# A tuned gated mix of attention and spectral filter: recalibrated scheduler durations, zero matmuls in TensorE gaps, gate column inside the value projection, 65-row last chunk

## The chip, the cores and the metric

The kernel runs on one core of one Trainium2 chip. Times are device microseconds of a whole execution. Before the change: 541.3 us, the median of three runs (541.14 to 542.06). The profiled span, about 2 us shorter than the time, is that of the traced execution.

Executions of one kernel do not all agree here. Each run comes with a state: "slow" when it is over 1.5% above the fastest run of the same kernel, "fast" otherwise.

## The reference, cut to what matters

```python
x = A_x                                             # 1 x 2048 x 448, bf16
g = sigmoid((x * gate_w).sum(-1, keepdims=True))    # the gate: one number per token
a = attention(x, wqkv, wo)                          # 16 heads of 28
b = irfft2(rfft2(B=x) * (w_r + 1j*w_i))             # over tokens and channels, as matmuls
return g * a + (1 - g) * b
```

The channel dimension of 448 is read by TensorE in four chunks of rows: 128, 128, 128 and 64.

## The kernel before

A scheduler in Python simulates the engines with assumed durations and emits instructions in the order that this simulation gives. The chip then runs each engine's list in order; no time of the simulation is enforced. Attention scores go to two tiles of PSUM of 3 and 2 banks, a bank for the 512 columns of one score matmul (128x1536 and 128x1024 in the profile), and ScalarE takes the exponentials of each (366 large ones). "Background" work (projections, the DFT, and some exponentials as a VectorE polynomial) shares two more banks.

```python
LAT = {"PE": 0.25, "ACT": 0.22, "DVE": 0.12, ...}   # us from an end to the start of a user
SWITCH = 0.17                                       # assumed us between two matmuls of different `mode`
...                                                 # cut
def v_block(self, g, b, due, wop, rel=0.0):         # value projection of 4 x 128 tokens
    for t in range(4):
        for c in range(4):
            n = 128 if c < 3 else 64
            ... mm(bank[:, 112*t:112*t+112], xT[b][0:n, c, 128*t:128*t+128], W[0:n, c, o0:o0+112])
            ops.append(self.pe(112, f, ..., dur=0.065))
...
def gate_item(self, due):                           # 64 matmuls of one column
    for t in range(NT):
        for c in range(4):
            n = 128 if c < 3 else 64
            ... mm(bank[:, t:t+1], xT[t//4][0:n, c, ...], self.wvr[0:n, c, 336:337])
...
e = self.act(0.1 + 512 * len(st) / 1200.0, ...)     # assumed time of one exponential
...
o = self.pe(0, fm, deps, tk + 2.0, mode="col", name="pv", dur=0.27 * len(pair))
```

Three kinds of matmuls alternate, which the code calls modes: scores use 32 rows of the array (`32*128` in the timeline; four heads side by side), the products with V ("PV") 32 columns (`128*32`), and everything else is "full". xT, the transposed input, has a row of ones behind its 448 channels, so its last chunk can be read 65 rows deep; the q and k projections already do that.

The softmax here doesn't subtract the row's maximum and nothing guards it: scores larger than these inputs give would overflow.

## Time and profile before

| | before |
|---|---|
| time, median | 541.3 us |
| profiled span | 537.2 us |
| TensorE busy, ScalarE busy | 89%, 80% |
| mean granted TensorE clock | 0.82 |
| chain of waits | TensorE 44%, VectorE 23%, ScalarE 18% |

These are lines of the profile page of the kernel before: busy time by engine; two rows of the 40 slices of the span (each digit is the busy share, or the granted clock, in tenths); and the chain that ended last.

```profile
PE 475.7 (89%) x3250; PEld 166.4 (31%) x3250; DVE 405.7 (76%) x678; ACT 430.7 (80%) x390; POOL 24.0 (4%) x56
...
ACT  2796777889939978987996987876797788999960
...
PEclk9997555899999968855987575559997996999986
...
PE 44%; DVE 23%; ACT 18%; issue 8%; DMA 4%; SPq 2%; ACTq 0%; DVEq 0%
```

The digits of the clock row fall to 5 in whole groups of slices, and ScalarE's digits are mostly lower there. Next, the windows view of the kernel before (columns: stretch, its length, busy time of each engine with instruction counts, granted clock, DMA share, GB/s):

```profile
40.00:60.00 20.00, 18.78 (x105) 5.15 (x105) 11.38 (x18) 12.98 (x12) 0.25 (x1) 0.68 0.01 2
60.00:80.00 20.00, 20.00 (x100) 5.15 (x100) 8.05 (x14) 14.71 (x13) 0.00 (x0) 0.50 0.06 14
80.00:100.00 20.00, 20.00 (x127) 6.79 (x123) 9.03 (x15) 13.20 (x13) 0.00 (x0) 0.54 0.03 8
140.00:160.00 20.00, 18.51 (x137) 7.49 (x136) 18.91 (x29) 11.89 (x14) 2.04 (x3) 1.00 0.01 4
```

There are two kinds of loss. From 60 to 80 us TensorE is busy for all 20 us at half clock, and ScalarE, which should be the bound, is busy for 14.71. From 140 to 160 us the clock is full, yet ScalarE is busy for 11.89 us only: value and q/k projections hold TensorE.

The timeline of TensorE before (start, duration, engine, line, operation, tiles, shapes, count, and in brackets the idle time before it and what ended it), first around 13 us, then from 37 us on:

```profile
13.02 1.05 PE L465 MATMUL bg<-cst,xtok 128*128 128x128 bf16 x16
...
37.83 1.69 PE L462 MATMUL bg<-wv,xT 128*128 128x112 bf16 x16
...
44.46 0.39 PE L462 MATMUL psA<-q,k 32*128 32x512 bf16 x2 [0.33 <-DMA k<-nrow]
```

Sixteen full-height transposes of 128 columns take 1.05 us; sixteen value matmuls, with fewer columns, take 1.69. The single starts in the trace show where: 49 ns from one 128-row matmul to the next, but about 145 ns into a 64-row one and 152 ns out of it, so some 96 to 103 ns extra each way, called a crossing below. In the same trace the q and k projections, whose last chunk is 65 rows deep, have no such step: at full clock their matmuls of 512 columns start 215 to 227 ns apart, into and out of a 65-row one as between 128-row ones.

### The profile page before, as it was taken

How to read it: one execution, taken by the hardware profiler on the slowest of the kernel's cores; microseconds unless marked ns; L12 is line 12 of the kernel's file. 1: busy time of each engine (PE TensorE's matmuls, PEld its weight loads, DVE VectorE, ACT ScalarE, POOL GpSimd, SP SyncE). 2: the span in 40 equal slices, each digit the busy share in tenths (PEclk: the TensorE clock that was granted, in tenths of full speed). 3: DMA queues.
4: the chain of work that ended last, by engine and by line, in shares of the span. 5: the costliest groups of instructions: out<-in, count | busy, mean ns of one | idle time of the engine just before them, and what ended most of it. 6: DMA issues, size and time to landing. Idle time of an engine off the chain costs nothing.

```text
span 537.2 us, 8484 instructions
## 1 busy us (share of the span) xinstructions
PE 475.7 (89%) x3250; PEld 166.4 (31%) x3250; DVE 405.7 (76%) x678; ACT 430.7 (80%) x390; POOL 24.0 (4%) x56
## 2 busy tenths in 40 slices
PE   7899999999998898799989989997879889888674
PEld 3343223333343322212333332322334333332121
DVE  2534722857989999997998988879896979798422
ACT  2796777889939978987996987876797788999960
POOL 5500000000010000000200000000000000000000
PEclk9997555899999968855987575559997996999986
DMA  8010010021000111111012000000000010010011
GB/s 237 2 55 1 2 23 9 1 56 22 2 4 1 42 42 40 24 34 37 16 23 52 13 1 2 2 10 11 13 13 11 23 29 22 21 36 19 20 35 36
DMA packets 27881, 13.98 MB, mean 26 GB/s; under 512 B 17248, under 2 KB 27456, under 8 KB 27840
## 3 DMA queue, kind: packets, MB, share of 16 engines
q1 hardware_dynamic: 26736, 13.09, 9.4%
q10 hardware_dynamic: 1104, 0.35, 0.3%
q8 instruction: 25, 0.41, 0.3%
q14 instruction: 16, 0.13, 0.1%
HBM read 11.21 MB, written 1.84 MB: 24 GB/s over the span
## 4 chain that ended last, share of the span: by engine, by line
PE 44%; DVE 23%; ACT 18%; issue 8%; DMA 4%; SPq 2%; ACTq 0%; DVEq 0%
PE bg L462 21%; ACT ring L980 18%; PE pvb L462 8%; PE psA L462 7%; PE psB L462 6%; DVE y L916 4%; DVE dW L931 2%; PE bg L465 2%; DVE dW L938 2%; SPq L444 2%; DVE y L942 2%; DVE dF L923 1%; DVE dW L927 1%; DMA k<-nrow 1%; DVE q L755 1%
## 5 line engine op out<-in xcount | busy, mean ns | idle before, releaser
L980 ACT ACTIVATE ring<-psA 128x1536 bf16<-128x1536 f32 (+1 forms) x184 | 274.1, 1490 | 52.3 <-PE psA L462 27.8
L980 ACT ACTIVATE ring<-psB 128x1024 bf16<-128x1024 f32 x183 | 195.3, 1067 | 20.1 <-PE pvb L462 7.1
L462 PE MATMUL psA<-q,k 32*128 32x512 bf16 x550 | 86.9, 451 | 26.0 <-ACT ring L980 23.6
L462 PEld LDWEIGHTS <-k 32*128 32x128 bf16 x1024 | 47.9, 93 | 155.2 <-issue 142.7
L916 DVE TENSOR_SCALAR y<-bg 128x512 uint16<-128x512 f32 x108 | 72.2, 683 | 20.6 <-PE bg L462 17.9
L462 PE MATMUL psB<-q,k 32*128 32x512 bf16 x366 | 84.2, 448 | 3.8 <-ACT ring L980 2.1
L462 PE MATMUL pvb<-ring,vw 128*32 128x512 bf16 x916 | 84.6, 458 | 1.3 <-DVE pvs L1070 0.7
L462 PE MATMUL bg<-q,k 32*128 32x512 bf16 x108 | 46.0, 447 | 3.8 <-DVE y L916 1.7
L462 PEld LDWEIGHTS <-xT 128*128 128x128 bf16 (+1 forms) x384 | 28.0, 101 | 43.4 <-issue 34.7
L938 DVE TENSOR_TENSOR dW<-dW,dF 128x2048 f16<-128x2048 f16 x27 | 32.9, 1217 | 0.2
L931 DVE TENSOR_TENSOR dW<-dF,dW 128x2048 f16<-128x2048 uint16 x27 | 32.8, 1216 | 0.2
L462 PEld LDWEIGHTS <-vw 128*32 128x32 bf16 x1024 | 19.4, 101 | 43.5 <-issue 39.9
L942 DVE TENSOR_TENSOR y<-y,dW 128x2048 uint16<-128x2048 uint16 x27 | 32.7, 1213 | 0.1
L462 PE MATMUL bg<-R,X 128*113 128x256 bf16 x128 | 31.2, 344 | 0.5 <-DVE U L1174 0.2
L462 PE MATMUL bg<-wvr,xT 128*128 128x112 bf16 (+3 forms) x256 | 30.1, 216 | 0.6 <-ACT w L810 0.3
L1174 DVE CAST U<-bg 113x512 bf16<-113x512 f32 x32 | 21.9, 687 | 7.3 <-PE bg L462 6.9
L815 POOL CAST vw<-w 128x16 bf16<-128x16 f32 x16 | 9.8, 628 | 388.4 <-ACT w L810 388.4
L1149 DVE CAST X<-bg 128x450 bf16<-128x450 f32 x16 | 10.0, 626 | 20.7 <-PE bg L462 20.7
L462 PE MATMUL bg<-Bd,xT 128*128 128x450 bf16 x64 | 25.4, 483 | 0.3 <-DVE y L916 0.2
L462 PE MATMUL bg<-xT,wpq 128*128 128x512 bf16 (+1 forms) x60 | 21.4, 447 | 2.2 <-DVE q L755 1.9
L462 PEld LDWEIGHTS <-X 128*113 128x113 bf16 x128 | 16.7, 157 | 19.5 <-issue 19.2
L462 PE MATMUL bg<-xT,wpk 128*128 128x512 bf16 (+1 forms) x60 | 20.6, 435 | 0.7 <-DVE y L916 0.4
(92 smaller groups left out, 458.8 us busy)
## 6 DMA issues: line engine op xcount, KB each, us to landing
RB<-cRB SPq DMA_DIRECT2D x16, 128.0 KB
Wg<-in_B_w_i_dram SPq DMA_DIRECT2D x32, 56.2 KB
xtok<-in_A_x_dram SPq DMA_DIRECT2D x4, 448.0 KB
out_dram<-fin SPq DMA_DIRECT2D x16, 112.0 KB
CS<-cCS SPq DMA_DIRECT2D x16, 96.0 KB
Wg<-in_B_w_r_dram SPq DMA_DIRECT2D x16, 56.2 KB
r<-rhl SPq DMA_DIRECT2D x32, 4.0 KB
U<-in_A_wqkv_dram SPq DMA_DIRECT2D x2, 252.0 KB
```

The source lines that it names most:

```text
L444: self.pin(e.dma_start(out=out() if callable(out) else out, in_=in_() if callable(in_) else in_))
L462: self.pin(self.nc.tensor.matmul(out, lhsT=lhsT, rhs=rhs, start=start, stop=stop, **kw))
L465: self.pin(self.nc.tensor.transpose(out=out, in_=in_, identity=self.c("ident")[0:n, 0:n]))
L755: self.pin(nc.vector.tensor_scalar(out=dst, in0=self.bgi(it), scalar1=self.sv, scalar2=None, op0=ALU.mult))
L815: self.pin(nc.gpsimd.tensor_copy(out=free_dims(self.vw[g][:], [[128, 4], [32, 4]], 4 * b * 128 + DH), in_=self.w[g][:, 4 * b:4 * b + 4, :]))
L916: self.pin(nc.vector.tensor_scalar(out=ys[:, s, :], in0=self.bgi(it), scalar1=127 * UNITS + 1.5, scalar2=0.0, op0=ALU.add, op1=ALU.max))
L931: self.pin(nc.vector.tensor_tensor(out=fl(self.dW), in0=fl(self.dF), in1=fl(self.dW), op=ALU.mult))
L938: self.pin(nc.vector.tensor_tensor(out=fl(self.dW), in0=fl(self.dW), in1=fl(self.dF).bitcast(F16), op=ALU.mult))
L942: self.pin(nc.vector.tensor_tensor(out=fl(ys), in0=fl(ys), in1=fl(self.dW), op=ALU.add))
L980: self.pin(nc.scalar.activation(out=self.ring[:, u0:u0 + len(st), :], in_=slot[:, 0:len(st), :], func=ACT.Exp, scale=LN2 / UNITS))
L1149: self.pin(nc.vector.tensor_copy(out=self.X1[:, t, :], in_=self.bgi(it)[:, 0:F2]))
L1174: self.pin(nc.vector.tensor_copy(out=dst, in_=src))
```

## The change

The intent, as the code shows it: give the simulation durations nearer the chip's; put zero matmuls ("fillers") on TensorE where the simulation finds it idle and its busy share of the last 3.4 us under 0.62; take the gate as a 113th column of one value block; and read the last chunk 65 rows deep, with a zero row in the weights, so that the crossings between 128-row and 64-row matmuls go.

```diff
-LAT = {"PE": 0.25, "ACT": 0.22, "DVE": 0.12, "POOL": 0.15, "SP": 2.1, "AQ": 2.1}
-SWITCH = 0.17
+LAT = {"PE": 0.26, "ACT": 0.22, "DVE": 0.15, "POOL": 0.15, "SP": 2.1, "AQ": 2.1}
+SWITCH = 0.1
+HAMW, HAMF = 3.4, 0.62
@@ the scheduler's loop @@
+        def fill(t):
+            gap = 0.35
+            so = scores.get(nexts)
+            if so is not None and ndep[so] == 0:
+                gap = min(gap, rdy[so] - t)
+            n = min(512, int((gap - SWITCH) * 2400.0) // 32 * 32)
+            if n < 96 or share(t) >= HAMF:
+                return False
+            ...                     # into a free background bank, or added into the open PV sum
                 if best is None:
+                    if e == "PE" and t > 8.0:
+                        f = fill(t)
@@ the filler @@
+        if bank is None:
+            self.mm(self.pv[:, 0:n], self.zero[:, 0:P], self.zero[:, 0:n], False, False)
+        else:
+            self.mm(self.bgt[bank][:, 0:n], self.zero[:, 0:P], self.zero[:, 0:n], True, True)
@@ value block (and the first DFT likewise) @@
-                n = 128 if c < 3 else 64
+                n = 128 if c < 3 else 65
-                ops.append(self.pe(112, f, deps + ops[-1:], due - 1.5, dur=0.065, ...
+                ops.append(self.pe(112, f, deps + ops[-1:], due - 1.5, dur=0.052, ...
+        m = 113 if g == 1 else 112          # the gate column rides in group 1
@@ gate_item: the 64 matmuls are gone, four small copies by VectorE collect the column @@
@@ exponentials, PV products @@
-            e = self.act(0.1 + 512 * len(st) / 1200.0, ...
+            e = self.act(0.052 + 512 * len(st) / 1200.0, ...
-                o = self.pe(0, fm, deps, tk + 2.0, mode="col", name="pv", dur=0.27 * len(pair))
+                o = self.pe(0, fm, deps, tk + 2.0, mode="col", name="pv", dur=0.225 * len(pair))
```

The instruction listing after the change holds 85 fillers with 36,288 columns (15.1 us at the 2.4 columns per ns that the code assumes). The first stands after 224 of the 916 score matmuls; 20 stand behind the last one.

More of the change, by code (lines that the diff above doesn't have):

```diff
@@ L249, in run, with share @@
         dq = list(dunits)
+        pvopen = [False]
+        pebusy = []
+        self.nfill = 0
+        def share(t):
+            a = t - HAMW
+            while pebusy and pebusy[0][1] <= a:
+                pebusy.pop(0)
+            return sum(e - max(s, a) for s, e in pebusy) / HAMW
+        def fill(t):
[6 more added lines that the diff above has]
+                return False
+            bl = [b for b in range(nbg_tiles) if held[b] is None and banks[b] <= t + 1e-9]
+            if bl:
+                target = bl[0]
+                banks[target] = t + SWITCH + n / 2400.0
+            elif pvopen[0]:
+                target = None
+            else:
+                return False
+            o = Op("PE", n / 2400.0, lambda: self.filler(target, n), (), 0.0, 0.0, "full", None, None, None, "fill")
+            o.start = t + (SWITCH if mode not in (None, "full") else 0.0)
+            o.end = o.start + o.dur
+            order.append(o)
+            pebusy.append((o.start, o.end))
+            self.nfill += 1
+            return o.end
         def finish(o, t0, dur):
             nonlocal left
+            if o.eng == "PE":
+                pebusy.append((t0, t0 + dur))
+                if o.name == "pv":
+                    pvopen[0] = not o.n
             o.start, o.end = t0, t0 + dur
@@ L295, in run @@
                 if best is None:
+                    if e == "PE" and t > 8.0:
+                        f = fill(t)
+                        if f:
+                            free[e], mode = f, "full"
+                            progress = True
                     continue
@@ L372, in build @@
         self.background()
+        self.sc.filler = self.filler
         order = self.sc.run(2, self.dunit_ops, 1)
@@ L396, in alloc @@
         self.wvr = T([P, 4, 337], BF16, "wvr")
+        self.WV0 = {1: 0, 2: 113, 3: 225}
         self.wo_pad = [T([P, D], BF16, f"wo{g}") for g in range(4)]
@@ L499, in plan_steps @@
             T.append(t)
-            t += 0.1 + 512 * len(st) / 1200.0
+            t += 0.052 + 512 * len(st) / 1200.0
         self.T, self.Tend = T, t
@@ L646, in weights @@
         K = -4000.0
-        self.wvd = {0: self.wload(self.wv0, 2 * D, 0, 112, K, "SP")}
+        z1 = self.pool(0.05, lambda: self.pin(nc.gpsimd.memset(self.wv0[64:65, 3, :], 0.0)), (), -4600)
+        z2 = self.pool(0.05, lambda: self.pin(nc.gpsimd.memset(self.wvr[64:65, 3, :], 0.0)), (), -4450)
+        self.wvd = {0: self.wload(self.wv0, 2 * D, 0, 112, K, "SP") + [z1]}
         for b in range(1, 4):
@@ L662, in weights @@
             rw[w] = [d1, d2]
-        dv = self.wload(self.wvr, 2 * D, 112, 336, K + 11, "SP", lat=4.0)
-        g1 = self.dma(self.wvr[:, 0:3, 336:337], self.gw[0:384].rearrange("(c p o) -> p c o", p=P, o=1), (), K + 12,
+        dv = (self.wload(self.wvr[:, :, 0:112], 2 * D, 112, 112, K + 11, "SP", lat=4.0)
+              + self.wload(self.wvr[:, :, 113:337], 2 * D, 224, 224, K + 11.5, "SP", lat=4.0))
+        g1 = self.dma(self.wvr[:, 0:3, 112:113], self.gw[0:384].rearrange("(c p o) -> p c o", p=P, o=1), (), K + 12,
                       dur=0.3, lat=8.0)
-        g2 = self.dma(self.wvr[0:64, 3, 336:337], self.gw[384:448].rearrange("(p o) -> p o", o=1), (), K + 12.1,
+        g2 = self.dma(self.wvr[0:64, 3, 112:113], self.gw[384:448].rearrange("(p o) -> p o", o=1), (), K + 12.1,
                       dur=0.2, lat=8.0)
         for g in range(1, 4):
-            self.wvd[g] = dv + [g1, g2]
+            self.wvd[g] = dv + [g1, g2, z2]
         for g in range(1, 4):
@@ L698, in bgi, with filler @@
         return t if dt == F32 else t.bitcast(dt)
+    def filler(self, bank, n):
+        if bank is None:
+            self.mm(self.pv[:, 0:n], self.zero[:, 0:P], self.zero[:, 0:n], False, False)
+        else:
+            self.mm(self.bgt[bank][:, 0:n], self.zero[:, 0:P], self.zero[:, 0:n], True, True)
     def x_block(self, b, due):
@@ L824, in v_block, with fg @@
         W = self.wv0 if g == 0 else self.wvr
-        o0 = 0 if g == 0 else 112 * (g - 1)
+        o0 = 0 if g == 0 else self.WV0[g]
+        m = 113 if g == 1 else 112
         for t in range(4):
             for c in range(4):
-                n = 128 if c < 3 else 64
+                n = 128 if c < 3 else 65
                 def f(t=t, c=c, n=n):
-                    self.mm(self.bgi(it)[:, 112 * t:112 * t + 112], self.xT[b][0:n, c, 128 * t:128 * t + 128],
-                            W[0:n, c, o0:o0 + 112], c == 0, c == 3)
+                    self.mm(self.bgi(it)[:, m * t:m * t + m], self.xT[b][0:n, c, 128 * t:128 * t + 128],
+                            W[0:n, c, o0:o0 + m], c == 0, c == 3)
                 deps = [self.xev[b, cc] for cc in range(4)] + self.wvd[g] + [wop[0]]
-                ops.append(self.pe(112, f, deps + ops[-1:], due - 1.5, dur=0.065, acq=it if not ops else None, rel=rel))
+                ops.append(self.pe(112, f, deps + ops[-1:], due - 1.5, dur=0.052, acq=it if not ops else None, rel=rel))
+        pre = []
+        if g == 1:
+            def fg():
+                self.pin(nc.vector.tensor_copy(out=self.glog[:, 4 * b:4 * b + 4],
+                                               in_=free_dims(self.bgi(it), [[m, 4]], 112)))
+            pre = [self.dve(0.08, fg, ops[-1:], due - 1.5)]
+            self.glops.append(pre[0])
         def fe():
-            src = self.bgi(it)[:, 0:448].rearrange("p (t s d) -> p t s d", t=4, s=4)
+            src = free_dims(self.bgi(it), [[m, 4], [DH, 4], [1, DH]])
             wv = free_dims(self.w[g][:], [[4, 4], [1, 4], [0, DH]], 16 * b)
@@ L840, in fe @@
                                              in0=src, in1=wv, op=ALU.mult))
-        e = self.dve(0.56, fe, [ops[-1], wop[0], self.vms[g], ("vwar", g)], due - 1.5, free=it)
+        e = self.dve(0.54, fe, [ops[-1], wop[0], self.vms[g], ("vwar", g)] + pre, due - 1.5, free=it)
         self.vready[g, b] = [e, wop[1]]
@@ L845, in gate_item @@
         nc = self.nc
-        it = Item()
-        ops = []
-        for t in range(NT):
-            for c in range(4):
-                n = 128 if c < 3 else 64
-                def f(t=t, c=c, n=n):
-                    self.mm(self.bgi(it)[:, t:t + 1], self.xT[t // 4][0:n, c, 128 * (t % 4):128 * (t % 4) + 128],
-                            self.wvr[0:n, c, 336:337], c == 0, c == 3)
-                deps = [self.xev[3, 3]] + self.wvd[1]
-                ops.append(self.pe(64, f, deps + ops[-1:], due, dur=0.06, acq=it if not ops else None, rel=due - 10))
-        e = self.act(0.15, lambda: self.pin(nc.scalar.activation(out=self.ge[:], in_=self.bgi(it)[:, 0:NT],
-                                                                func=ACT.Exp, scale=-1.0)), ops[-1:], -9.0, free=it)
+        e = self.act(0.08, lambda: self.pin(nc.scalar.activation(out=self.ge[:], in_=self.glog[:], func=ACT.Exp,
+                                                                 scale=-1.0)), self.glops, -9.0)
         a = self.dve(0.09, lambda: self.pin(nc.vector.tensor_scalar(out=self.ge[:], in0=self.ge[:], scalar1=1.0,
                                                                     scalar2=None, op0=ALU.add)), (e,), due)
-        b = self.dve(0.12, lambda: self.pin(nc.vector.reciprocal(out=self.gs[:], in_=self.ge[:])), (a,), due)
+        b = self.dve(0.16, lambda: self.pin(nc.vector.reciprocal(out=self.gs[:], in_=self.ge[:])), (a,), due)
         self.gate_op = self.dve(0.09, lambda: self.pin(nc.vector.tensor_scalar(
@@ L869, in attention @@
         self.vready = {}
+        self.glops = []
         rate = (ts[1] - ts[0]) / 16.0
@@ L981, in fe @@
                                               func=ACT.Exp, scale=LN2 / UNITS))
-            e = self.act(0.1 + 512 * len(st) / 1200.0, fe, [m] + exps[-1:], i * .001, name="exp")
+            e = self.act(0.052 + 512 * len(st) / 1200.0, fe, [m] + exps[-1:], i * .001, name="exp")
             e.step = i
@@ L1021, in fm @@
                                     pi == 0 and qi == 0, last and qi == len(pair) - 1, tile_position=(0, 32 * s))
-                o = self.pe(0, fm, deps, tk + 2.0, mode="col", name="pv", dur=0.27 * len(pair))
+                o = self.pe(0, fm, deps, tk + 2.0, mode="col", name="pv", dur=0.225 * len(pair))
+                o.n = pi == len(pairs) - 1
                 prev_pv = o
@@ L1124, in background @@
         dI = self.dma(free_dims(self.Binv[:], [[D, 4], [1, D]]), dr["Binv"].ap(), (), -98, rel=40.0, lat=5.0)
-        self.gate_item(60.0)
+        self.gate_item(ts[4] + 5.0)
         cost = 0.0
@@ L1139, in background @@
             for c in range(4):
-                n = 128 if c < 3 else 64
+                n = 128 if c < 3 else 65
                 def f(c=c, n=n, t=t, it=it):
```

## The prediction

> **What bounds the kernel now.** 541.3 us on one core; the profiled span is 537.2. ScalarE's exponentials are the floor: 366 of them, in a steady full-clock stretch one pair (3+2 banks) per about 2.3 us, so some 415 us plus about 16 us of start and 16 us of tail. They last from 15.5 to 521 us: some 90 us are lost (page: ScalarE 80% busy, TensorE 89%; chain of waits: TensorE 44%, ScalarE 18%). Two causes. (1) The granted clock averages 0.82; the windows view shows only 1.00 and 0.50, some 190 us at half. From 52 to 96 us TensorE is busy without a break at 0.50 and ScalarE only about 70% of the time. A bank of exponentials costs about 0.52 us at full clock, 0.62 at half. (2) Group changes even at full clock: at 152 to 160 us three value projections and the q/k projections hold TensorE for about 8 us while ScalarE waits; smaller holes at 39, 372 and 405 us.
>
> [...]throttled stretches last whole multiples of 3.41 us. Weighing matmul columns by used rows and columns, I estimate that the clock falls after windows under about 0.35 of full-clock capacity, and comes back only after a window over about 0.75 of half-clock capacity: the same work per window.
>
> **What the change does.**
> - 65-row last chunk. Timeline: sixteen 112-column value matmuls take 1.69 us; sixteen 128-row transposes 1.05. Single starts: 49 ns inside 128-row runs, about 145 into and 148 out of a 64-row matmul. With 65 rows I expect the 64-row penalty gone: about 0.19 us for each of 64 value groups and 16 first-DFT tiles, so 15 us of TensorE time; a value block falls to about 0.9 us.
> - Gate column. 64 one-column matmuls go (about 4 us with their switches, in the throttled, TensorE-bound stretch at 60 to 72 us); four small VectorE copies come.
> - Fillers. 85 zero matmuls stand in the new order, 60 in the body (about 10 us at full clock, 2%), 25 around the tail; none before a quarter of the scores, so the throttle of 48 to 98 us has none. Zero data warmed the clock in the prologue. Nothing paces a filler: it runs when reached, so tail fillers run early.
> - New durations reorder work.
>
> **On the critical path.** About half of the 19 us of removed TensorE time (10 us). Throttling at half clock costs about 0.10 us on each of 291 banks, 29 us; I expect half the throttled time to go, 14 us, partly by fillers, partly because the same columns in less time are denser.
>
> **Prediction: 516 us, 8 in 10 between 498 and 533.** Faster by over 2%: 0.83; within 2%: 0.13; slower: 0.04.
>
> **Right if:** value blocks at about 0.9 us; the hole near 152 us about 3 us shorter; mean clock about 0.9; ScalarE's busy share about 84%. **Wrong step shown by:** clock still near 0.82 (fillers misplaced, since the scheduler's full-clock times are not the chip's); TensorE waits in front of fillers; value blocks still 1.7 us.
>
> **What would make it wrong.** Removing slow switches leaves TensorE idler and throttles it more; a new order that is worse in VectorE-bound stretches (160 to 215 us, VectorE 96% busy); or the clock staying full, giving under 500.

The windows of the estimate are stretches of 3.41 us of the trace before. 541 us, less 10 and less 14, is 517, given as 516. What it says of zero data in the prologue, in numbers: in the trace before, ten zero matmuls of 512 columns start from 1.31 us on, 427 ns apart, transposes follow at 5.55 us, and the full clock begins at 6.19 us. In the trace after, eight of the ten and no other matmul had started on TensorE when the full clock began, at 4.62 us; the last two start 217 ns apart.

## The result, and the profile after

483.58 us, median of four runs (482.0 to 486.83), against 541.22 for the kernel before in the same rounds. The ratio is 0.8944, with a 95% interval of 0.8885 to 0.9003. Ratios here are the mean time of one kernel's fast runs over that of the other's of the same rounds, so not quite the ratio of the medians. The change is faster by over 10%, and the time lies below the predicted range of 498 to 533.

| | before | after |
|---|---|---|
| profiled span | 537.2 us | 482.2 us |
| ScalarE busy | 80% | 88% |
| mean granted clock | 0.82 | 0.943 |
| sixteen value matmuls | 1.69 us | 0.98 us |
| end of the last exponential to the end | 16.0 us | 17.4 us |

The same lines of the page after:

```profile
PE 425.6 (88%) x3271; PEld 156.5 (32%) x3271; DVE 401.2 (83%) x682; ACT 423.8 (88%) x390; POOL 22.5 (5%) x58
...
ACT  2679999779999969999999989689999979999950
...
PEclk9989999759999958999999999599999999999998
...
ACT 38%; PE 28%; DVE 15%; issue 13%; DMA 4%; SPq 2%; ACTq 0%; DVEq 0%
```

The chain has turned over: ScalarE 38% and TensorE 28%, where TensorE had 44 and ScalarE 18. The windows view after, at the same times (the value projections of the second group, from 153 us on before, now run from about 123 to 145 us):

```profile
40.00:60.00 20.00, 18.41 (x157) 6.37 (x155) 13.27 (x23) 19.25 (x19) 0.25 (x1) 1.00 0.02 3
60.00:80.00 20.00, 18.81 (x130) 5.89 (x129) 17.46 (x28) 20.00 (x19) 0.00 (x0) 1.00 0.18 44
80.00:100.00 20.00, 18.25 (x110) 4.24 (x107) 13.15 (x24) 17.01 (x15) 0.00 (x0) 0.75 0.02 2
120.00:140.00 20.00, 18.08 (x194) 8.96 (x196) 16.12 (x29) 20.00 (x22) 0.91 (x3) 1.00 0.08 16
140.00:160.00 20.00, 16.75 (x157) 7.16 (x156) 19.97 (x40) 20.00 (x20) 0.80 (x1) 1.00 0.09 20
```

The half-clock stretch of 47 to 98 us (score matmuls 55 to 130) is gone, although no filler stands there; a shorter one comes later in the program, at 90 to 107 us (score matmuls 150 to 175). ScalarE is busy without a break through the group change where it had lost over 7 us. In the value blocks after, the single starts at full clock are 49 ns into a 65-row matmul and 53 ns out of it: the crossings have gone. TensorE's timeline after, a value block, then some fillers:

```profile
239.16 0.98 PE L508 MATMUL bg<-wvr,xT 128*128 128x112 bf16 x16
```

```profile
218.36 0.25 PE L508 MATMUL bg<-zero 128*128 128x192 bf16 x1
218.74 0.39 PE L508 MATMUL psB<-q,k 32*128 32x512 bf16 x2
219.06 0.82 PE L508 MATMUL bg<-zero 128*128 128x512 bf16 x3
220.08 0.39 PE L508 MATMUL psA<-q,k 32*128 32x512 bf16 x3 [0.20 <-ACT ring L1033]
220.41 0.28 PE L508 MATMUL bg<-zero 128*128 128x256 bf16 x1
221.00 0.39 PE L508 MATMUL psB<-q,k 32*128 32x512 bf16 x2 [0.31 <-ACT ring L1033]
221.32 0.98 PE L508 MATMUL bg<-zero 128*128 128x512 bf16 x4
222.34 0.40 PE L508 MATMUL psA<-q,k 32*128 32x512 bf16 x3
```

Here the fillers fall into time in which TensorE would have waited for ScalarE: the scores behind two of the four groups still wait 0.20 and 0.31 us for an exponential, and those behind the other two start within 0.15 us.

### Two readings of the traces that the experiments use

**The clock fell after stretches with few columns.** In the traces before and after, only the clocks 1.00 and 0.50 occur, and every half-clock stretch but the last, which the end cuts off, lasts a whole number of 3.41 us (1 to 15 before, 1 to 5 after), and so does every full-clock one. I cut the traces at that grid and counted, in each window of 3.41 us, the matmul columns, weighed by the share of array rows and columns in use (a measure of mine; some matmul records are missing). Before: of 11 windows after which the clock fell during the exponentials, 10 had at most 0.35 of the full-clock capacity; of 82 at full clock after which it stayed, 3 had. (The traces of a_nofill, a_fill16 and b_dur_65, below, counted in the same way, give 38 falls, all after windows of at most 0.39 and 34 of them of at most about 0.35.) The clock mostly came back after windows of about 0.7 or more of half-clock capacity, which is about the same number of columns, though such a window did not always suffice: a recount of the trace before gives 11 windows after which it came back, 10 of them at 0.69 to 0.97, and 43 after which it did not, 11 of them at 0.69 to 0.75. In the longest half-clock stretch, 51 us from 47 us on, TensorE was busy for all of the 38 us from 60 to 98 us. No long idle gap was needed: the clock fell at 47 us although the longest idle gap of TensorE in the window before was the 0.33 us shown above. In the trace after, about ten windows (9 to 11, by how a matmul across a border is counted) stayed at full clock that would have been under 0.355 without the fillers' columns.

**Two numbers per run.** Each run lists its span and its mean clock, so its time at half clock is 2 x (1 - clock) x span: 193 us in the profile before, 55 after (the half-clock stretches of the two traces add up to 195 and 56). A straight line with one slope for all kernels and one intercept for each fits the 155 runs that list a clock with a spread of 0.7 to 2.7 us per kernel. (One run of the kernel before is left out: its listed clock of 0.677 does not fit its time of 535.9.) The slope is 0.29 us of time per us at half clock. Fast and slow runs of one kernel lie on the same line (they differ by 0.3 us on average), and so do the runs of the kernel before on all four chips (within 1 us). But the slope is not the same for all: the 50 runs of the kernel before alone give 0.24, the kernels built on the changed one 0.34 together, with standard errors of 0.01. The intercept, "time at an equal clock" below, is an estimate worked out from these runs with the common 0.29; it is a way to put a number on what is left when the clock is taken out. Between kernels with about the same half-clock time it hardly depends on the slope; where two differ by 100 us of half-clock time, a slope of 0.24 or 0.34 instead shifts their difference by 5 us either way.

### The profile page after: what moved, and what is told of

The parts are those of the page before. It is cut to its first block, busy times and chain, and to the rows that moved or that the text cites. A ratio compares the mean times of both kernels' runs of the same rounds, so it can differ in the third digit from the quotient of the medians.

```text
span 482.2 us, 8537 instructions
## 1 busy us (share of the span) xinstructions
PE 425.6 (88%) x3271; PEld 156.5 (32%) x3271; DVE 401.2 (83%) x682; ACT 423.8 (88%) x390; POOL 22.5 (5%) x58
## 4 chain that ended last, share of the span: by engine, by line
ACT 38%; PE 28%; DVE 15%; issue 13%; DMA 4%; SPq 2%; ACTq 0%; DVEq 0%
ACT ring L1033 37%; PE bg L508 13%; PE psA L508 5%; PE pvb L508 5%; PE psB L508 4%; DVE y L969 2%; SPq L490 2%; PE bg L511 2%; DVE dW L984 1%; DMA k<-nrow 1%; DMA U<-in_A_wqkv_dram 1%; DVE dF L976 1%; DMA r<-rhl 1%; DMA rs<-pvs 1%; DVE pvs L1124 1%
## 5 line engine op out<-in xcount | busy, mean ns | idle before, releaser
L1033 ACT ACTIVATE ring<-psA 128x1536 bf16<-128x1536 f32 (+1 forms) x184 | 283.8, 1542 | 22.7 <-PE psA L508 16.4
L1033 ACT ACTIVATE ring<-psB 128x1024 bf16<-128x1024 f32 x183 | 205.6, 1124 | 6.9 <-PE pvb L508 4.2
L508 PE MATMUL psA<-q,k 32*128 32x512 bf16 x550 | 76.9, 400 | 25.6 <-ACT ring L1033 22.0
L508 PE MATMUL psB<-q,k 32*128 32x512 bf16 x366 | 75.3, 397 | 6.7 <-ACT ring L1033 5.3
L508 PE MATMUL pvb<-ring,vw 128*32 128x512 bf16 x916 | 73.4, 400 | 0.5 <-DVE pvs L1124 0.5
L508 PEld LDWEIGHTS <-xT 128*128 128x128 bf16 x320 | 18.5, 97 | 16.1 <-issue 14.3
L810 DVE TENSOR_SCALAR k<-bg,cst 128x512 bf16<-128x512 f32 x15 | 11.2, 749 | 13.7 <-PE bg L508 13.7
L1160 DVE SCALAR_TENSOR_TENSOR fin<-bg,gs,xtok 128x448 bf16<-128x448 f32 x16 | 10.9, 680 | 10.9 <-PE bg L508 10.8
L508 PE MATMUL bg<-Bd,xT 128*128 128x450 bf16 x64 | 17.2, 357 | 2.1 <-DVE X L1203 1.0
L976 DVE TENSOR_SCALAR dF<-y 128x2048 uint16<-128x2048 uint16 x27 | 18.5, 686 | 0.3
```

The source lines that it names most:

```text
L508: self.pin(self.nc.tensor.matmul(out, lhsT=lhsT, rhs=rhs, start=start, stop=stop, **kw))
L810: self.pin(nc.vector.tensor_scalar(out=dst, in0=self.bgi(it), scalar1=self.sv, scalar2=None, op0=ALU.mult))
L976: self.pin(nc.vector.tensor_scalar(out=fl(self.dF), in0=fl(ys), scalar1=511, scalar2=None, op0=ALU.bitwise_and))
L1033: self.pin(nc.scalar.activation(out=self.ring[:, u0:u0 + len(st), :], in_=slot[:, 0:len(st), :], func=ACT.Exp, scale=LN2 / UNITS))
L1160: self.pin(nc.vector.scalar_tensor_tensor(out=fin[:], in0=self.bgi(it)[:, 0:D], scalar=self.gs[:, t:t + 1], in1=self.bm[:, t, 0:D], op0=AL ...
```

## The experiments

The scheduler's order is sensitive: a change of 0.002 us in one assumed latency moves 3,000 lines of the order. So, wherever possible, an edit was made at emission only, and the listing was compared to be sure that nothing else moved ("same order"). Theories at the start: "switch" (the 64-row crossings), "clock" (the fillers), "order" (the new durations).

Summary. "Fast ratio" is against the kernel before of the same rounds, given where at least two fast runs exist. Half-clock time and time at an equal clock are means over all runs of the kernel.

| kernel | runs | time, us | fast ratio | half clock, us | at an equal clock, us |
|---|---|---|---|---|---|
| before | 50 | 530 to 551 | | 204 | 480.2 |
| before, 65 rows (b_65) | 4 | 524 to 544 | | 215 | 475.0 |
| before, new durations (b_dur) | 4 | 526 to 548 | 0.978 | 209 | 470.7 |
| before, both (b_dur_65) | 6 | 505 to 524 | 0.947 | 168 | 461.5 |
| after, fillers of 16 columns (a_fill16) | 6 | 501 to 514 | 0.942 | 163 | 461.0 |
| after, no fillers (a_nofill) | 4 | 491 to 512 | | 154 | 459.1 |
| after, no fillers, 64 rows (a_64_nofill) | 6 | 516 to 526 | 0.969 | 178 | 468.2 |
| after, 64 rows (a_64) | 4 | 491 to 512 | 0.915 | 84 | 473.4 |
| after | 4 | 482 to 487 | 0.894 | 63 | 465.6 |

### b_65: the kernel before with 65 rows, same order

```diff
-                n = 128 if c < 3 else 64      # value blocks and first DFT
+                n = 128 if c < 3 else 65      # and row 64 of wv0, wvr set to zero
```

> The kernel before, same order of instructions on TensorE, with the last chunk of the value projection and of the first DFT read 65 rows deep instead of 64 (the extra weight row is zero). Theory 'switch' (the 64-row penalty sat on the chain of waits and is worth about its full TensorE time): 541 falls to 520 to 528, sixteen value matmuls take about 0.9 us instead of 1.69. Theory 'clock' (fillers carry the gain): under 8 us gained here, 533 to 541. Theory 'order' (the new durations carry it): the same, 533 to 541.

Measured: 523.61, 541.61, 542.54 and 543.8 us. The one fast run has a clock of 0.848; the others 0.78 to 0.785. At an equal clock it gains 5 us of the 15 us of crossings, and the half-clock time does not fall. The one fast run lies in the range that "switch" named, but by its clock: at 0.848 the lines of the kernel before (slopes 0.29 and 0.24) give 526 to 529 us. The "switch" theory as stated fails: in the old order most of the freed TensorE time is not kept.

### b_dur: the kernel before with the new durations alone

```diff
-SWITCH = 0.17
+SWITCH = 0.1
-... dur=0.065 (value matmul) ... 0.1 + (exponential) ... dur=0.27 (PV)
+... dur=0.052 (value matmul) ... 0.052 + (exponential) ... dur=0.225 (PV)
```

(LAT and two VectorE durations as in the change.)

> The kernel before with the new durations in the scheduler alone: no filler, 64 rows, gate matmuls kept. Theory 'order': most of the 58 us comes here, 541 falls to 500 to 510. Theory 'switch': little or nothing, since the new durations of a value matmul are true only with 65 rows: 532 to 545. Theory 'clock': 532 to 545, mean clock stays near 0.82.

Measured: 525.93, 526.45, 526.48 (fast) and 547.59 us; fast ratio 0.9779. About 12 us, so neither "nothing" nor "most". The clock is no better (0.814 in the fast runs); at an equal clock it is 9.5 us.

### a_nofill: the changed kernel without fillers, same order

```diff
-            o = Op("PE", n / 2400.0, lambda: self.filler(target, n), ...
+            o = Op("PE", n / 2400.0, lambda: None, ...
```

> The changed kernel with the same order of all other instructions, the 85 fillers left out. Theory 'clock': most of the gain goes, 515 to 540, and the clock falls from 0.94 to about 0.85. Theories 'switch' and 'order': the fillers are worth at most a third, 484 becomes 486 to 503.

Measured: 490.71, 501.53, 511.64 and 511.88 us at clocks of 0.887 to 0.826. The median, 506.58, is 23 us above the changed kernel (the best run, the only fast one by the rule, 7 us), and the executions scatter by 21 us where the changed kernel's scatter by 5. That lies between the two expectations (515 to 540, and at most 503): the fillers carry a large part, not most. The clock is what "clock" expected. With one fast run this is weak by itself; a_fill16 below, with three, settles it.

### a_64: the changed kernel with 64 rows, same order and fillers

> The changed kernel, order and fillers the same, with the last chunk back at 64 rows. Theory 'switch': 484 becomes 500 to 515. Theories 'clock' and 'order': 484 becomes 486 to 495, since TensorE has room at full clock.

Measured: 491.0, 493.95, 493.97 (fast) and 512.23 us. The fast runs are about 10 us above the changed kernel, as "clock" and "order" expected; at an equal clock 7.8. Sixteen value matmuls are back at their old time, in the timeline of this kernel:

```profile
236.93 1.70 PE L508 MATMUL bg<-wvr,xT 128*128 128x112 bf16 x16
```

### b_dur_65: the kernel before with new durations and 65 rows

The same order as b_dur, with the 65-row edit of b_65.

> The kernel before with the new durations and 65 rows, in the same order as the run with the new durations alone; gate matmuls kept, no fillers. At an equal clock I expect 7 to 10 us less than the run with the new durations alone (526): fast runs 510 to 519. If 65 rows were worth their full 15 us and gave clock too: under 508. If the gate column carries much, this stays over 10 us slower at an equal clock than the changed kernel without fillers (489 at 0.887, 500 at 0.848).

Measured: 504.79 to 512.01 (five fast), 524.08 us; fast ratio 0.9465. Against b_dur, in the same order, the 65 rows give 9.2 us at an equal clock and 40 us less at half clock (20 to 25 us less in the changed order, a_64 and a_64_nofill). So the two parts work together. A likely reason, not shown by itself: the new durations say that a value matmul takes 0.052 us; measured, it is 0.061 with 65 rows (0.98 us for sixteen) and 0.106 with 64 (1.69). And this kernel is within about 2 us of the changed kernel without effective fillers (next), which bounds what the gate column and the rest give.

### a_fill16: the same fillers, 16 columns each

```diff
-lambda: self.filler(target, n)
+lambda: self.filler(target, 16)
```

> The changed kernel, same order, every one of the 85 fillers still there but streaming 16 columns instead of 96 to 512: the instructions, their weight loads and their few waits stay, the array activity goes. If fillers work by activity alone (clock theory): like the kernel without fillers, fast runs 490 to 510, clock 0.83 to 0.89. If they work in some other way (as spacers, by the waits they carry): near 484, clock near 0.93.

Measured: 500.97 to 513.55 us, median 509.44; clock 0.827 to 0.86. All 85 instructions, weight loads and waits are there, and the gain is not. It is the columns that count: 163 us at half clock, against 63 with the full columns, all of them zeros, in the same order. The clock rows of the pages: this kernel's (a slow execution at 0.829), and that of b_dur_65 (a fast one, also at 0.829):

```profile
PEclk9999999999995957565755655669999969999887
```

```profile
PEclk9959976999996597978755759896999869697887
```

In the first, the clock holds over the first twelve slices, in which the changed kernel has almost no fillers either, and then breaks down for half the span, where the changed kernel's row above shows nines with a few short falls.

### a_hamf75 and a_hamf90: more fillers

```diff
-HAMW, HAMF = 3.4, 0.62
+HAMW, HAMF = 3.4, 0.75        # 167 fillers;   0.90: 288 fillers
```

> The changed kernel with the filler threshold at 0.75 of the window instead of 0.62: 167 fillers instead of 85, and an order that differs. Theory 'clock' with room left: mean clock 0.95 or above, half-clock time from 55 to about 30 us, time 474 to 482. If fillers cost more TensorE time than they save: 484 to 490 at a higher clock.

> The same with the threshold at 0.90: 288 fillers. If the clock is all that matters: clock 0.97 or above and 468 to 478. If fillers now stand in the way of score matmuls (each up to 0.21 us, no pacing): slower than with 167, 480 to 490, with a high clock.

Measured: 469.0 to 484.16 us (median 474.12, fast ratio 0.8787) and 471.74 to 476.89 us (median 475.07, fast ratio 0.8858). Half-clock time 39 and 17 us, time at an equal clock 463.7 and 469.6 us. Both beat the kernel before and, by their medians, the changed kernel by about 9 us; the interval of a_hamf75's ratio (0.8695 to 0.8879) lies just below the changed kernel's, that of a_hamf90 (0.8787 to 0.8928) overlaps it. Both have another order than the changed kernel, and another order alone moves the median by up to 7 us (a_pert2, below): the fall of the half-clock time, 63 to 39 to 17 us, goes with the fillers, but a gain of 9 us is hardly more than luck of the order. The second expectation of a_hamf90 (slower, by more of them standing in the way) came only in part: at an equal clock it is about 6 us above a_hamf75, in another order, and it gets them back in clock. Its six runs scatter by 5 us, those of a_hamf75 by 15. The clock row of its page (fast, span 475.1):

```profile
PEclk9999999999999999999977987999999999999999
```

### a_64_nofill: no fillers and 64 rows, the changed kernel's order

> The changed kernel, same order, without fillers and with 64 rows: what is left of the change is the order (new durations) and the gate column. Half-clock time 160 to 200 us. If 65 rows are worth the same with and without fillers (7 to 10 us at an equal half-clock time): 512 to 520 at 170 us of half clock, against 507 to 512 without fillers at 65 rows. If the 64-row switches were mostly hidden: under 511.

Measured: 516.27 to 526.4 us, fast ratio 0.9693, 178 us at half clock. Against a_nofill, the 65 rows are worth 9.1 us at an equal clock without fillers, against 7.8 with them (a_64): the expectation of 7 to 10 held.

### b_gate: the kernel before without 48 of the 64 gate matmuls

The gate is wrong on purpose here (and the output was reported wrong); the order of all else is the same.

```diff
-                    self.mm(... self.wvr[0:n, c, 336:337], c == 0, c == 3)
+                    if c == 0:
+                        self.mm(... self.wvr[0:n, c, 336:337], True, True)
```

> The kernel before, same order, with 48 of the 64 gate matmuls left out (the gate is wrong on purpose, from the first 128 of 448 products; all 16 of its 64-row matmuls are among those left out). They stand on TensorE between 56 and 72 us, at half clock, where it is never idle. Theory of the prediction: 3 to 4 us less at an equal half-clock time, 534 to 538. If the removed time is lost again (later in the group or in the clock): 538 to 545, no change.

Measured: 534.54 to 547.2 us, fast ratio 1.0014 (0.9903 to 1.0125). At an equal clock 1.2 us less, which is inside the scatter. The 3 to 4 us are not shown.

### a_pert1 and a_pert2: another order for no reason

```diff
-LAT = {"PE": 0.26, ...       and       "DVE": 0.15
+LAT = {"PE": 0.262, ...      and       "DVE": 0.148
```

> The changed kernel with one assumed latency 0.262 us instead of 0.26: no better information, but another order (3,900 lines of the order listing differ) and 84 fillers. It measures what luck of the order is worth. If the gain is the mechanism's: 478 to 494. If this order was a lucky one: over 500.

> The same with VectorE's assumed latency 0.148 instead of 0.15, 75 fillers. If the gain is the mechanism's: 478 to 494, the clock 0.91 to 0.95. If this order was a lucky one: over 500, the clock below 0.9.

Measured: 473.47 to 490.62 us (median 485.05; one fast run by the rule, since its best run is far ahead) and 483.22 to 499.02 us (median 490.39, fast ratio 0.9066). At an equal clock 465.0 and 461.8, against 465.6; half-clock time 67 and 100 us against 63. So luck of the order is worth up to about 4 us at an equal clock and some 40 us of half clock the other way; between the medians that leaves 7 us. The gain is not luck, but its last 7 us or so may be.

### b_pert1 and b_durx: scatter and parts of the old order

```diff
-LAT = {"PE": 0.25, ...
+LAT = {"PE": 0.252, ...                             # b_pert1
-... 0.1 + (exponential), dur=0.27 (PV)
+... 0.052 + (exponential), dur=0.225 (PV)           # b_durx, nothing else
```

> The kernel before with one assumed latency 0.252 instead of 0.25: another order (3,000 lines of the listing differ) for no reason. If the order's scatter is small: 533 to 547, on the line of the kernel before within 4 us. If the scatter is as large as the 9 us put down to the new durations, that gain is not shown.

> The kernel before with only the durations of exponentials (0.1 to 0.052 us overhead) and of PV products (0.27 to 0.225 us) new. If these carry the order's 9 us: fast runs 524 to 532 at 195 us of half clock. If the latencies, the mode-change time and the value block matter as much: 532 to 540.

Measured: b_pert1 536.07 to 549.99 us, fast ratio 1.0011, 0.7 us under the kernel before at an equal clock. b_durx 536.84 to 556.13 us, fast ratio 1.0066, 4.3 us above it. The exponential and PV durations alone do not give b_dur's 9.5 us, and cost something. Which of the new durations do (latencies, mode-change time, value block, or all together) is open.

### b_fill and b_fill512: unplanned fillers in the old order

```diff
             self.mm(slot[:, e, :], ... scores ...)
+            if i % 2 == 0 and self.pvopen:       # 156 times
+                self.mm(self.pv[:, 0:256], self.zero[:, 0:P], self.zero[:, 0:256], False, False)
```

(512 columns in b_fill512.)

> The kernel before, same order, with 156 zero matmuls of 256 columns (16.6 us at full clock), one after every second group of score matmuls while the PV sum is open: fillers that no scheduler has planned. If the clock itself costs 0.29 us per us at half clock in the old order too: half-clock time falls from 206 to 80 to 150 us and the time from 540 to 515 to 532, on a line about 5 us above the kernel before's (480 + 0.29 x half-clock time). If the price is only 0.15: 535 to 545. If unplanned fillers cost their full time: 545 to 560.

> The same with 512 columns (33 us of TensorE time at full clock). Clock price 0.29: half-clock time under 80 us, time 500 to 522, line some 10 to 15 us above. Clock price 0.15 or full filler cost: 540 to 560.

Measured: b_fill 534.97 to 554.98 us, fast ratio 1.0015. The clock rose (149 us at half, from 204), and the time did not fall: at an equal clock it is 17.7 us above the kernel before, about the full 16.6 us of its filler columns (16.8 at the 216 ns per 512 columns of the trace after). My 5 us were wrong by a factor of three. b_fill512: 523.37 to 548.11 us, fast ratio 0.9789, 110 us at half clock, 24 us above at an equal clock, of 33 us of columns. Within b_fill alone, its seven runs have a slope of 0.29 (0.24 in the kernel before), so time at half clock has a price of that order in the old order as well. The fillers of the changed kernel, placed where the scheduler saw a gap, cost 4.6 us (465.6 against 461.0 of a_fill16) for 15.1 us of columns; with slopes of 0.24 to 0.34 that is nothing to 9 us, so it is below the full price, and not known better.

### a_notail and a_75_notail: no fillers behind the last scores

> The changed kernel, same order, without the 20 fillers after the last score matmul. If they stand in the way: the stretch from the last exponential to the end falls from 17.4 to 15.5 to 16.5 us, the time by about 1 us. If they keep the clock up for the last output matmuls: the stretch grows by 1 us or more. Either way the time is within 2 us of the changed kernel's at an equal half-clock time.

> Threshold 0.75 and no tail fillers. 468 to 477, as the run with threshold 0.75 within 2 us; half-clock time 25 to 65 us as there. Faster than the changed kernel by 6 to 14 us.

TensorE's timeline at the end of the changed kernel shows what was at stake:

```profile
465.14 2.33 PE L508 MATMUL bg<-zero 128*128 128x512 bf16 x10
471.33 0.39 PE L508 MATMUL bg<-r,cst 8*128 8x512 bf16 x1 [3.86 <-DMA r<-rhl]
471.65 1.34 PE L508 MATMUL bg<-zero 128*128 128x512 bf16 x4
472.78 3.10 PE L508 MATMUL bg<-wo,q 128*128 128x448 bf16 x8
```

The ten fillers meant to bridge the wait for the DMA run at once, and TensorE then stands idle for 3.86 us. Measured: a_notail 481.35 to 493.4 us, fast ratio 0.9054; the stretch after the last exponential is 16.9 us instead of 17.4. a_75_notail 471.46 to 490.57 us, fast ratio 0.8992, worse than a_hamf75 by its median (485.98 against 474.12) through more half-clock time (65 against 39 us) at the same 464 us. Leaving the tail fillers out is no gain that these runs show, and a_75_notail missed its expectation. Its order is that of a_hamf75 but for the tail; why its runs have more half-clock time is open (the scatter of executions alone may be it).

## Why the prediction was wrong

The direction, the two causes and most signs were right, and the sum was short by more than half: 25 us predicted, 58 measured. The signs it named came, stronger than named: value blocks at 0.98 us, a clock of 0.926 to 0.943 (0.9 named), ScalarE 88% busy (84% named), and no hole left in ScalarE at the group change. What it listed as the way to be wrong, "the clock staying full, giving under 500", is nearly what happened.

The sum as measured, on the path before, b_dur, b_dur_65, a_fill16, after (means over all runs; the parts are estimates from the fitted lines):

| step | time at an equal clock | half-clock time, times 0.29 |
|---|---|---|
| new durations | -9.5 us | +1.3 us |
| 65 rows | -9.2 us | -11.8 us |
| gate column and the rest | -0.5 us | -1.7 us |
| fillers' columns | +4.6 us | -29.0 us |
| sum | -14.6 us | -41.2 us |

How a step divides between the two columns depends on the slope: with 0.24 the sums are about -22 and -34 us, with 0.34 about -8 and -48. The fast ratios of the same kernels (0.978, 0.947, 0.942, 0.894) need no slope: new durations 12 us, 65 rows 17, gate column and the rest 2, fillers' columns 26, of 541.

- **The step that failed: the price and the amount of throttled time.** The prediction said: "Throttling at half clock costs about 0.10 us on each of 291 banks, 29 us; I expect half the throttled time to go, 14 us". The runs show 0.24 us (the kernel before alone) to 0.29 us (all kernels) for each us at half clock, so some 49 to 59 us for the 204 us of before, and 141 us of it gone, 69%: 34 to 41 us where the prediction had 14. Both factors were too small; the price was 29 us over some 180, or 0.16 per us. The likely error, by the numbers of the traces, was in the baseline. I compared a bank of exponentials at half clock (0.62 us) with the average at full clock in the same trace (0.52), but that average held the group-change holes: at full clock the median time from one exponential to the next is 0.452 us per bank in that very trace. The changed kernel's full-clock stretches run at 0.471 per bank. ScalarE's own floor, which the code's new durations put at 512/1200 + 0.052/2.5 = 0.447 us (an estimate, close to the steady pair of five banks per 2.3 us in the trace before), gives 0.17 us on each of 291 banks: 50 us over 180 us, or 0.28 per us, inside what the runs show.
- **Fillers.** That they count by their columns was right (a_fill16: 163 us at half clock with 16 columns each, 63 with all), and that they would be few and cheap. That half of the throttling would go was an unsupported guess: I had estimated from the trace before that the clock falls under 0.35 of capacity, but did not ask how far below it the windows were. They are just below, most of them 0.26 to 0.35, so by estimate a few hundred columns make up the difference (at 216 ns per 512 columns, 3.41 us hold about 8,090, and 0.05 of that is about 400).
- **65 rows.** The 15 us of crossings and half of them on the path were right: 7.8 to 9.2 us at an equal clock in the changed order. A value block of 0.9 us was nearly right (0.98). Missed: with the new durations it also takes 40 us off the half-clock time (20 to 25 in the changed order); in the old order it does not.
- **Gate column.** Predicted as 4 us of TensorE time of the 19, with half of the 19 on the path. b_gate shows nothing beyond scatter.
- **New durations.** The prediction gave them no number. They are worth 9.5 us at an equal clock, more than three changes of the order for no reason moved it (0.6, 3.8 and 0.7 us), though a part of them alone (b_durx) made it 4.3 us worse.
- **Tail.** The prediction gave it no number; the stretch behind the last exponential grew by 1.4 us in the profiled runs. The warning that nothing paces a filler was right (ten of them run at 465.14 us, and TensorE then stands idle for 3.86 us).
- **"Removing slow switches leaves TensorE idler and throttles it more"**, named as a risk, did not come: the half-clock time fell wherever the new durations were there too. In the old order it was 215 against 204 us (b_65), which is no more than a change of the order for no reason gave (b_pert1, 216).

What stays open: which of the new durations matter, what decides whether an execution lands at the high or the low end of its kernel's clock (the grid of 3.41 us begins with the first full clock, at 6.19 us in the trace before and 4.62 us in the trace after, so where it lies is a candidate; no run here varies that alone), and the exact weights of the measure of columns.

## What to carry to other kernels

Price a throttled stretch against the bound engine's floor, not against the average of the unthrottled stretches, which hold their own losses; and list span and clock of every run, since a line through them separates a change of the clock from a change of the work, as well as its slope is known. Here, where the clock fell mostly after windows just under 0.35 of capacity, a few planned dummy columns in real gaps were worth more than they cost (15 us of columns, 26 us of net gain), while a like number outside gaps cost about what they saved (b_fill). After an edit that makes an operation faster, try new durations in whatever orders the work together with it: here, by the means over all runs, neither of the two alone gave half of what both gave (2 and 8 us, against 29), though which of the durations did it is open.
